# Gated product interleaved with a linear-attention recurrence: the split of x one step later, and a 0-3-3-2 pattern of gate halves

## The chip, the cores and the metric

The kernel runs on one core of one Trainium2 chip. The metric is device time in microseconds (us); of several runs the median is given. Engines are named as in the profile: PE (matrix products), PEld (its weight loads), DVE (vector), ACT (scalar), POOL (GpSimd), SP (the queue that issues most DMAs; ACT issues some as well).

## What is computed

There are 32 sequences (4 batches of 8 heads) of 768 positions and head size 48. Per sequence a recurrence with a decay per key channel is run, and its output, regrouped to 3072 tokens of 384 values, goes through a product of two linear maps and two more linear maps:

```python
for t in range(S):
    state = alpha[:, :, t, :, None] * state + np.einsum('bhd,bhe->bhde', k[:, :, t], v[:, :, t])
    y[:, :, t] = np.einsum('bhd,bhde->bhe', q[:, :, t], state)
...
x = y.transpose(0, 2, 1, 3).reshape(B * S, H * D)      # 3072 x 384
h = (x @ w1) * (x @ w2) @ w3                           # 1024 wide
out = h @ w_out                                        # 3072 x 384
```

## The kernel before

**Phase one** is the loop over `n` (steps 0 to 24). The 768 positions of a batch are six chunks of 128, so four batches make 24 chunks, one per step, for all eight heads at once. In step n PE does `attend_state(n - 1)` (L349), `scores(n)` (L330), `transposed(n + 1)` (L290), `attend(n - 1)` (L355), `outer(n)` (L302, not in a batch's last chunk) and `decays(n + 3)` (L253 or L256). ACT takes logarithms (L238), exponentials (L259, L260), copies transposed q and k out of PSUM (`qkT`, L292), copies the output y (L359) and issues its stores to the DRAM tile `xd` (L365). DVE masks the scores (`ms`, L333), scales q and k (`qk`, L268) and adds up states (L310, L312). Inputs are loaded three to five steps ahead by SP (L124, L130, L131, L136).

**Groups and gates.** Three chunks make a group g of 384 tokens. Once they are stored, `load_x(g)` (L370) brings them back transposed as `xT`, and `split_x(g, 0)` makes three parts `x3` of it: one ACT instruction (L376) and two DVE instructions (L377, L378), on 128x1152 elements each. There is one buffer of `xT`, and one of `x3` in phase one. `gate(g, f)` is one of eight column tiles of the product (x w1)(x w2): two halves, each `exact(...)` with six matmuls (L387), a copy on ACT (L389), three matmuls (L391) and a DVE instruction (L392); behind the second half DVE multiplies the two (`ab`, L403) and SP stores an earlier result (L410). The generators of gates stand in the queue `fill`, and `run(k)` emits k halves at its place in the step.

**Weights** arrive as 64-bit floats and are converted by generators that `convert(steps)` advances: a DMA into `raw` (L181), ACT instructions L189, L194 and L207, DVE instructions L190, L193, L196, L197, L199, L209 and L210. They fill ACT and DVE beside the recurrence.

**Order.** `begin = {4: group 0, 8: group 1, ... 20: group 4}` says in which step x of a group is loaded. For groups 0 to 3 four of the eight gates are put into `fill`, for group 4 all eight. The framework puts the instructions of each engine into one in-order stream by its own planning, so that an instruction can stand on its engine earlier or later than in the source; PSUM has eight banks, which all steps take in turn (`bank()`).

**Phase two** starts behind the loop: what is left in `fill`, then the remaining gates of all groups, with the conversion and folding of w3 and w_out (L430, L436), then 24 output tiles (`project`, L387 and L391 on `w3o`).

Of the kernel before, what the change touches and what calls it, by code (L numbers as in the profile page):

```python
# [48 lines left out]
def kernel(  # L49
# [71 lines left out]
    def load_a(n):  # L121
        if n < N:
            st["a", n] = inp.tile([C, H, D], FP32, tag="ac", name="ac")
            nc.sync.dma_start(out=st["a", n], in_=rows(alpha, n))  # L124

    def load_kq(n):
        if n >= N:
            return
        st["kq", n] = inp.tile([C, 2, H, D], FP32, tag="kq", name="kq")
        nc.sync.dma_start(out=st["kq", n][:, 0], in_=rows(k, n))  # L130
        nc.sync.dma_start(out=st["kq", n][:, 1], in_=rows(q, n))  # L131

    def load_v(n):
        if n < N:
            st["v", n] = vs[n % len(vs)]
            nc.sync.dma_start(out=st["v", n][:, :, 0:D], in_=rows(v, n))  # L136
# [77 lines left out]
    def convert(steps, ahead=3):  # L214

        for _ in range(steps):
            while weights and len(begun) < ahead:
                begun.append(weights.popleft())
                next(begun[-1])
            if not begun:  # L220
                return
            x = begun.popleft()
            try:
                next(x)
                begun.appendleft(x)
            except StopIteration:
                pass
# [5 lines left out]
    def logs(n):  # L233
        if n >= N:
            return
        a = st.pop(("a", n)).rearrange("p h d -> p (h d)")
        la = st["la", n] = work.tile([C, DM], FP32, tag="la", name="la")
        nc.scalar.activation(la, a, AF.Ln)  # L238
        if n >= LATE:

            t = st["la", n] = work.tile([C, 2, DM], FP32R, tag="la2", name="la2", bufs=1)
            nc.scalar.copy(t[:, 0], la)
            nc.vector.tensor_sub(t[:, 1], la, t[:, 0].bitcast(FP32))
        if n in ends:
            nc.scalar.dma_start(out=ends[n][2:3], in_=a[0:1])

    def decays(n):
        if n >= N:
            return
        lc = bank()[:, 0:DM]  # L250
        la = st.pop(("la", n))
        if n < LATE:
            nc.tensor.matmul(lc, utri if n % 2 else after, la, start=True, stop=True)  # L253
        else:
            for i in range(2):
                nc.tensor.matmul(lc, sums[:, n % 2], la[:, i], start=(i == 0), stop=(i == 1))  # L256

        e = st["e", n] = work.tile([C, 2, DM], FP32, tag="e", name="e", bufs=3)
        nc.scalar.activation(e[:, 0], lc, AF.Exp, scale=-1.0)  # L259
        nc.scalar.activation(e[:, 1], lc, AF.Exp)  # L260
        if n in ends:
            nc.scalar.dma_start(out=ends[n][0:1], in_=e[0:1, 0])
        if n + 1 in ends:
            nc.scalar.dma_start(out=ends[n + 1][1:2], in_=e[C - 1:C, 1])
# [14 lines left out]
    def transposed(n):  # L279
        if n >= N:  # L280
            return
        qk = qks[n % 3]
        qkT = work.tile([C, 2, NP, C], FP32, tag="qkT", name="qkT")

        tp = [bank().rearrange("p (i j c) -> p i j c", i=2, j=NP) for _ in range(2)]
        for i in range(2):
            for j in range(NP):
                for half in range(2):
                    s = ds(DP * half, DP)
                    nc.tensor.transpose(tp[half][:, i, j, :], qk[s, i, 2 * j:2 * j + 2, :], ident[s, s])  # L290
        for half in range(2):
            nc.scalar.copy(qkT[:, :, :, ds(DP * half, DP)], tp[half])  # L292
        st["qkT", n] = qkT
# [30 lines left out]
    def scores(n):  # L324
        qkT = st["qkT", n]
        sc = [bank().rearrange("p (j c) -> p j c", j=NP) for _ in range(2)]
        for j in range(NP):
            for i in range(2):
                r = ds(DP * i, D)
                nc.tensor.matmul(sc[i][:, j, :], qkT[r, 0, j, :], qkT[r, 1, j, :], start=True, stop=True)  # L330
        ms = work.tile([C, 2, NP, C], FP32, tag="ms", name="ms")
        for i in range(2):
            nc.vector.tensor_tensor(ms[:, i].bitcast(I32), sc[i].bitcast(I32), keep_bc, op=ALU.bitwise_and)  # L333
        st["ms", n] = ms
# [3 lines left out]
    def attend_state(n):  # L338
        qkT = st.pop(("qkT", n))

        y = [bank()[:, 0:HP * C].rearrange("p (j c) -> p j c", c=C) for _ in range(2)]
        st["y", n] = y, [(half * HP + j, i, y[i][ds(DP * half, DP), j, :])
                         for j in range(HP) for i in range(2) for half in range(2)]
        if n % NCH:
            for j, i, to in st["y", n][1]:
                r = ds(DP * i, D)
                nc.tensor.matmul(to, Ts[n % 2][r, j, :], qkT[r, 1, j, :],  # L349
                                 start=(j % HP == 0), stop=False, skip_group_check=True)  # L350
# [21 lines left out]
    def split_x(g, i):  # L372
        x = st.pop(("xT", g))
        t = tr[i].tile([C, 3, KM, TG], FP32R, tag="x3", name="x3")
        st["x3", g] = t
        nc.scalar.activation(t[:, 0], x, AF.Copy, scale=1.0 - 2.0 ** -13)  # L376
        nc.vector.tensor_sub(t[:, 1], x, t[:, 0].bitcast(FP32))  # L377
        nc.vector.scalar_tensor_tensor(t[:, 2], t[:, 0].bitcast(FP32), 1.0 + 1.0 / P, x,  # L378
                                       op0=ALU.mult, op1=ALU.subtract)

    def exact(to, w, x, scale):

        p1, p2 = (bank()[:, 0:to.shape[1]] for _ in range(2))
        n = len(w[0])
        for part in range(2):
            for i in range(n):
                nc.tensor.matmul(p1, w[part][i], x[part][i], start=(part == i == 0), stop=(part == 1 and i == n - 1))  # L387
        t = gw.tile(list(to.shape), FP32, tag="t", name="t")
        nc.scalar.activation(t, p1, AF.Copy, scale=(1.0 + 1.0 / P) * scale)  # L389
        for i in range(n):  # L390
            nc.tensor.matmul(p2, w[2][i], x[2][i], start=(i == 0), stop=(i == n - 1))  # L391
        nc.vector.scalar_tensor_tensor(to, p2, -scale, t, op0=ALU.mult, op1=ALU.add)  # L392

    def gate(g, f):
        r = []
        x = [[st["x3", g][:, part, kk, :] for kk in range(KM)] for part in range(3)]
        for i, scale in enumerate((1.0, P * P)):
            r.append(gw.tile([C, TG], FP32, tag="r", name="r"))
            exact(r[-1], [[w12[:, part, i, kk, ds(f * C, C)] for kk in range(KM)] for part in range(3)], x, scale)
            if len(r) == 1:  # L400
                yield
        ab = abp.tile([C, TG], FP32, tag="ab", name="ab")
        nc.vector.tensor_mul(ab, *r)  # L403
        store_ab()
        st["ab"] = g, f, ab

    def store_ab():
        if "ab" in st:
            g, f, ab = st.pop("ab")
            nc.sync.dma_start(out=abd[g][:, f, :], in_=ab)  # L410
# [57 lines left out]
    def run(pieces):  # L468

        for _ in range(pieces):  # L470
            if not fill:
                return
            try:
                next(fill[0])
            except StopIteration:
                fill.popleft()
# [18 lines left out]
    load_kq(3)  # L495
    load_a(4)

    begin = {4 + 4 * g: (g, range(FH if g < 4 else KF)) for g in range(5)}

    for n in range(N + 1):  # L500
        load_v(n + AHEAD - 1)
        load_a(n + 5)
        load_kq(n + AHEAD)
        if n:
            attend_state(n - 1)
        if n < N:
            scores(n)
        transposed(n + 1)
        if n - 1 in begin:
            g, tiles = begin[n - 1]  # L510
            split_x(g, 0)
            fill.extend(gate(g, f) for f in tiles)
        if n == 0:
            logs(2)
            decays(2)
            logs(3)
        early = n < 7
        convert(1, 2 if n == 0 else 3)
        advance(n)
        if n:  # L520
            attend(n - 1)
        outer(n)
        run(n - 1 not in begin)
        if early:
            convert(1)
        decayed(n + 2)
        logs(n + 4)
        if n in begin:
            load_x(begin[n][0], nc.scalar)
        convert(early and n > 2)  # L530
        run(1)
        decays(n + 3)
        load_ends(n + 2)
        convert(early or n % 3 == 0)
        run(n - 1 in begin)
    part1.close()


# [78 lines left out]
```

## Time and profile before

| | |
|---|---|
| median of 8 runs | 508.35 us (506.76 to 509.5) |
| profiled execution | 509.1 us |
| its span, first to last instruction | 507.3 us |
| mean granted PE clock | 0.966 |
| busy: PE, DVE, ACT | 467.7, 371.1, 248.4 us |
| HBM traffic | 56.40 MB read, 22.06 MB written |

A matmul's end is modelled, and matmuls overlap, so a busy PE is not PE at its peak. Busy shares are means over stages with different limits: phase one (to about 213 us) and phase two have to be read apart. In what follows, a row of a timeline gives start and length in us, the engine, the line of the kernel, the operation, output and inputs, shapes and the number of instructions merged; in square brackets stands the idle time of the engine just before and what ended it.

### The profile page before, as it was taken

To read this page: it belongs to the slowest core of one execution; us is meant where nothing else is said; L and a number is where in the kernel's file an instruction comes from. 1 tells how busy PE (TensorE), PEld (TensorE's weight loads), DVE (VectorE), ACT (ScalarE), POOL (GpSimd) and SP (SyncE) were. 2 spreads that over 40 slices of the span, in tenths; PEclk is the share of its full clock that TensorE was granted. 3 is DMA by queue.
4 is the path that set the end of the run, shared out by engine and by line. 5 is a ranking of instruction groups with operands and counts; after the bars stand their busy time and mean duration, and the time that the engine had idled before them with its cause. 6 is when DMAs were issued, how large, how long until landed. Compare 5 with 4: busy or idle time off the path is not lost.

```text
span 507.3 us, 9883 instructions
## 1 busy us (share of the span) xinstructions
PE 467.7 (92%) x3760; PEld 425.3 (84%) x3760; DVE 371.1 (73%) x620; ACT 248.4 (49%) x479; POOL 13.5 (3%) x43
## 2 busy tenths in 40 slices
PE   3778399499799999999999999999999999999997
PEld 1666288398698899899999998898888799999996
DVE  2778698699965767599999976967533496777771
ACT  2665566468656655355555554544323343333330
POOL 2000000010100000000000000000000000000000
PEclk9988599789899999999999999999999999999999
DMA  9999999998688843265555432332001686656511
GB/s 174 183 220 196 249 225 224 201 236 219 143 193 197 184 88 109 76 189 166 193 191 184 159 118 90 133 112 72 33 31 48 168 230 190 183 174 180 176 54 47
DMA packets 168735, 79.10 MB, mean 156 GB/s; under 512 B 112856, under 2 KB 162544, under 8 KB 168688
## 3 DMA queue, kind: packets, MB, share of 16 engines
q1 hardware_dynamic: 147184, 70.73, 54.3%
q10 hardware_dynamic: 21504, 7.75, 6.6%
q8 instruction: 29, 0.48, 0.4%
q14 instruction: 18, 0.15, 0.1%
HBM read 56.40 MB, written 22.06 MB: 155 GB/s over the span
## 4 chain that ended last, share of the span: by engine, by line
PE 66%; DMA 2%; ACT 2%; DVE 1%; issue 1%; ACTq 1%; DVEq 0%
PE bank L387 35%; PE bank L391 17%; PE bank L436 8%; PE bank L355 1%; PE bank L430 1%; PE bank L330 1%; DMA kq<-in_k_dram 1%; DMA raw<-in_moe_w_out_dram 1%; PE bank L349 1%; ACTq L365 1%; DVE x L378 1%; PE bank L290 0%; PE bank L302 0%; ACT qkT L292 0%; ACT t L389 0%
## 5 line engine op out<-in xcount | busy, mean ns | idle before, releaser
L387 PE MATMUL bank<-x,w 128*128 128x384 f32 x768 | 164.5, 349 | 18.1 <-ACT x L376 10.9
L387 PEld LDWEIGHTS bank<-x,w 128*128 128x128 f32 x768 | 136.6, 192 | 23.9 <-ACT x L376 11.3
L389 ACT ACTIVATE t<-bank 128x384 f32<-128x384 f32 x152 | 73.5, 490 | 119.1 <-PE bank L387 100.3
L392 DVE SCALAR_TENSOR_TENSOR r<-bank,t 128x384 f32<-128x384 f32 x128 | 68.8, 553 | 46.4 <-ACT t L389 37.2
L391 PE MATMUL bank<-x,w 128*128 128x384 f32 x384 | 89.6, 341 | 1.5 <-DVE x L378 1.4
L391 PEld LDWEIGHTS bank<-x,w 128*128 128x128 f32 x384 | 69.6, 192 | 3.1 <-PE bank L387 1.4
L387 PE MATMUL bank<-w3o,ab 128*128 128x384 f32 x384 | 70.6, 335 | 1.0 <-ACT ab L454 1.0
L387 PEld LDWEIGHTS bank<-w3o,ab 128*128 128x128 f32 x384 | 66.8, 188 | 1.4 <-ACT ab L454 1.3
L436 PE MATMUL bank<-wo,w3T 128*128 128x384 f32 x128 | 42.6, 486 | 0.0
L189 ACT ACTIVATE rest<-raw 128x512 f32<-128x512 uint32 (+1 forms) x36 | 23.4, 649 | 29.9 <-DMA raw<-in_moe_w_dram 17.1
L391 PE MATMUL bank<-w3o,ab 128*128 128x384 f32 x192 | 37.2, 334 | 0.0
L436 PEld LDWEIGHTS bank<-wo,w3T 128*128 128x128 f32 x128 | 24.2, 189 | 14.9
L403 DVE TENSOR_TENSOR ab<-r 128x384 f32<-128x384 f32 x64 | 35.4, 554 | 0.9
L455 DVE TENSOR_TENSOR ab<-abl,ab 128x1024 fp32r<-128x1024 f32 x24 | 29.3, 1222 | 8.6 <-ACT ab L454 8.6
L454 ACT ACTIVATE ab<-abl 128x1024 fp32r<-128x1024 f32 x24 | 25.5, 1062 | 20.1 <-PE bank L391 18.9
L333 DVE TENSOR_TENSOR ms<-bank,keep 128x512 int32<-128x512 int32 x48 | 31.2, 681 | 3.9 <-PE bank L330 3.9
L391 PEld LDWEIGHTS bank<-w3o,ab 128*128 128x128 f32 x192 | 33.6, 188 | 0.0
L330 PEld LDWEIGHTS bank<-qkT 48*128 48x128 f32 x384 | 24.7, 193 | 10.2 <-ACT qkT L292 4.8
L330 PE MATMUL bank<-qkT 48*128 48x128 f32 x384 | 29.8, 292 | 3.8 <-ACT qkT L292 3.3
L292 ACT COPY qkT<-bank 128x512 f32<-128x512 f32 x48 | 25.7, 586 | 13.9 <-PE bank L290 7.4
L392 DVE SCALAR_TENSOR_TENSOR o<-bank,t 128x384 f32<-128x384 f32 x24 | 13.4, 557 | 22.6 <-issue 12.9
L194 ACT ACTIVATE power<-power,rebias 128x512 uint32<-128x512 uint32 (+1 forms) x36 | 25.0, 695 | 9.9 <-DVE power L193 9.7
(65 smaller groups left out, 511.7 us busy)
## 6 DMA issues: line engine op xcount, KB each, us to landing
abd<-ab SPq DMA_DIRECT2D x64, 192.0 KB
abl<-abd SPq DMA_DIRECT2D x24, 512.0 KB
raw<-in_moe_w_dram SPq DMA_DIRECT2D x16, 512.0 KB
raw<-in_moe_w_dram SPq DMA_DIRECT2D x24, 256.0 KB
ac<-in_alpha_dram SPq DMA_DIRECT2D x24, 192.0 KB
kq<-in_k_dram SPq DMA_DIRECT2D x24, 192.0 KB
kq<-in_q_dram SPq DMA_DIRECT2D x24, 192.0 KB
v<-in_v_dram SPq DMA_DIRECT2D x24, 192.0 KB
```

The source lines that it names most:

```text
L194: nc.scalar.activation(power, power, AF.Relu, scale=2.0 ** 23, bias=rebias)
L292: nc.scalar.copy(qkT[:, :, :, ds(DP * half, DP)], tp[half])
L330: nc.tensor.matmul(sc[i][:, j, :], qkT[r, 0, j, :], qkT[r, 1, j, :], start=True, stop=True)
L333: nc.vector.tensor_tensor(ms[:, i].bitcast(I32), sc[i].bitcast(I32), keep_bc, op=ALU.bitwise_and)
L387: nc.tensor.matmul(p1, w[part][i], x[part][i], start=(part == i == 0), stop=(part == 1 and i == n - 1))
L389: nc.scalar.activation(t, p1, AF.Copy, scale=(1.0 + 1.0 / P) * scale)
L391: nc.tensor.matmul(p2, w[2][i], x[2][i], start=(i == 0), stop=(i == n - 1))
L392: nc.vector.scalar_tensor_tensor(to, p2, -scale, t, op0=ALU.mult, op1=ALU.add)
L403: nc.vector.tensor_mul(ab, *r)
L436: nc.tensor.matmul(po, w3T[:, j, :], wo[:, j, :], start=(j == 0), stop=(j == KF - 1))
L454: nc.scalar.activation(t[:, 0], ab, AF.Copy, scale=1.0 - 2.0 ** -13)
L455: nc.vector.tensor_sub(t[:, 1], ab, t[:, 0].bitcast(FP32))
```

## The change

The step in which x is split and its gates are put into the queue is n - 2, not n - 1, behind the load. In each step from 6 on, the number of gate halves follows from n: none in the split step, then three, three and two. Before it was two in every step. `run` is called at the same three places of the step.

```diff
-        if n - 1 in begin:
-            g, tiles = begin[n - 1]
+        if n - 2 in begin:
+            g, tiles = begin[n - 2]
             split_x(g, 0)
             fill.extend(gate(g, f) for f in tiles)
+        pieces = (0, 3, 3, 2)[(n - 6) % 4] if n > 5 else 0
...
         outer(n)
-        run(n - 1 not in begin)
+        run(pieces > 0)
...
         convert(early and n > 2)
-        run(1)
+        run(pieces > 1)
         decays(n + 3)
         load_ends(n + 2)
         convert(early or n % 3 == 0)
-        run(n - 1 in begin)
+        run(pieces > 2)
```

## The prediction

> **What bounds the kernel now.** I read the page first, then the time-sliced windows, the waits of PE, and last the timelines of PE, ACT and DVE around the waits that the change aims at.
>
> The page says that PE is busy for 467.7 of 507.3 us, and the windows say where the rest is.
>
> ```profile
> PE 467.7 (92%) x3760; PEld 425.3 (84%) x3760; DVE 371.1 (73%) x620; ACT 248.4 (49%) x479; POOL 13.5 (3%) x43
> ...
> 33.92:40.75 6.83, 5.61 (x54) 4.36 (x58) 6.83 (x12) 4.23 (x10) 0.00 (x0) 0.50 1.18 221
> 51.00:64.64 13.64, 5.52 (x13) 3.93 (x14) 9.08 (x15) 7.46 (x15) 0.00 (x0) 0.50 1.06 248
> 66.66:128.12 61.46, 54.31 (x656) 48.78 (x652) 53.75 (x99) 40.10 (x88) 3.44 (x6) 0.92 0.99 219
> 140.15:198.68 58.53, 57.46 (x755) 52.84 (x751) 40.05 (x68) 35.03 (x79) 3.18 (x9) 1.00 0.67 157
> 213.00:507.00 294.00, 289.70 (x1586) 271.53 (x1582) 215.10 (x348) 125.43 (x212) 0.00 (x0) 1.00 0.43 136
> ```
>
> Columns of a window: stretch, length, busy time of PE, PEld, DVE, ACT and POOL, granted PE clock, DMA share, GB/s. From 140 us on PE is full at clock 1.00: there only less PE work helps, and the change removes none. All that can be won lies before 140, where DVE (53.75 of 61.46) and the DMA engines (share 0.99) are nearly full too. The waits of PE and the timeline show what is lost:
>
> ```profile
> PE bank L387 <- ACT x L376: 10.9, 2, 9.7
> PE bank L387 <- DVE x L377: 7.2, 3, 4.9
> ...
> 48.01 1.09 PE L355 MATMUL bank<-ms,v 128*64 128x128 f32 x16
> 58.84 1.33 PE L387 MATMUL bank<-x,w 128*128 128x384 f32 x3 [9.73 <-ACT x L376]
> ...
> 94.07 0.79 PE L387 MATMUL bank<-x,w 128*128 128x384 f32 x3 [1.17 <-ACT x L376]
> 99.75 1.33 PE L387 MATMUL bank<-x,w 128*128 128x384 f32 x3 [4.89 <-DVE x L377]
> ...
> 134.07 0.79 PE L387 MATMUL bank<-x,w 128*128 128x384 f32 x3 [2.09 <-DVE x L377]
> 135.43 0.76 PE L391 MATMUL bank<-x,w 128*128 128x384 f32 x3 [0.57 <-DVE x L378]
> ...
> 167.64 0.76 PE L391 MATMUL bank<-x,w 128*128 128x384 f32 x3 [0.83 <-DVE x L378]
> ```
>
> In each group's split step the first gate half reaches PE before the split of x is done: 9.98 us for group 0 (9.73 and the 0.25 that follows at 60.41), 6.06 for group 1, 2.66 for group 2, 0.83 for group 3, none for group 4. After the first three the clock is 0.50, over 5.8, 5.85 and 3.4 us of PE work, which costs half of it: 2.9, 2.9 and 1.7. Together 27.0 us. That is the ceiling, not the gain, as two more lines show:
>
> ```profile
> 54.73 0.66 ACT L189 ACTIVATE rest<-raw 128x512 f32<-128x512 uint32 x1 [4.73 <-DMA xT<-xd]
> 57.12 0.61 ACT L292 COPY qkT<-bank 128x512 f32<-128x512 f32 x1
> 95.00 0.43 DVE L190 TENSOR_SCALAR mant<-raw 128x512 uint32<-128x512 uint32 x1 [4.23 <-DMA raw<-in_moe_w_dram]
> ```
>
> At the first stall ACT itself stands for 4.73 us, until a transfer has landed, and only then copies qkT of step 6 (done 57.73), which the scores of step 6 need whatever the gates do. At the second stall DVE stands for 4.23 us for a weight tile; the split at 98.35 is only behind that in its queue.
>
> **The change part by part.** Units, from the timeline of step 10 (105.77 to 113.09 us): a gate half is 1.67 and 1.56, mean 1.62 us of PE; a step without gates is 3.66 plus 0.44 for the sums of logarithms, 4.1 us. The split is ACT 1.17 and DVE twice 1.35 (starts 1.27 apart).
>
> *The split a step later.* No instruction is added or removed; the two DVE and one ACT instructions go behind one more step of recurrence on those queues, past its copies, its masks and its xd stores. The split issues no DMA; in the built order the load of x for group 1 also moves, from behind the e of step 7 to step 8, so it starts later by some of the slack won. SP and POOL lose or gain no instruction in phase one except that stores of ab move with their gates. From load to first gate half there is, in the source, about one step before and two and a half after.
>
> *The split step without gates.* Between the last gate of a group and the first of the next lie 4.1 us more of PE work, which covers the chain of 1.17 + 1.27 + 1.35 = 3.8 us that must wait for the single x3 buffer. With that cover gone it costs what it costs now (2.66 at group 2).
>
> *Three, three, two halves.* 8 halves per four steps stay 8, at 4.1 + 3 x 1.62 = 9.0 us of PE in a full step. Of group 4 three gates instead of four fit in phase one: 38 halves instead of 40, so two (3.24 us) are moved into phase two, which PE bounds; they are subtracted below. There five gates instead of four (16 us) stand ahead of the first split of phase two, which needs 3.8: no cost.
>
> *Sum up to the scores of step 13* (128.12 us now, 16 halves done; then T, 14 done; gain 128.12 - T - 3.24). The scores of step 6 start at 57.7 instead of 66.66. From there two bounds. DVE: its instructions of steps 6 to 12, at the distances of their starts, are 51.7 us in the new order (55.6 in the old: one split more, two weight conversions fewer); with the old idle time (63.6 us from the masks of step 6 to those of step 13, 55.9 busy, so 7.7 idle) from the end of the scores at 58.9 it is at step 13's masks at 118.3; less the old lag of 3.4 behind the scores, T = 114.9: gain 10.0. DMA at its old rate: 13.46 MB (219 GB/s x 61.46) plus 2.1 of the 8.9 us that are skipped (236 GB/s), less two weight tiles and one store, 1.1 MB, is 14.5 MB or 66 us: T = 123.8, gain 1.1. PE itself would need 7 x 4.1 + 14 x 1.62 = 51.4 us and is not the bound. I take 4.0, below the middle of the two, because the DMA share of 0.99 is nearer to full than DVE's 0.87.
>
> *Sum from step 13 on.* Groups 2 and 3 lose 2.66 + 1.7 + 0.83 = 5.2 and some 0.3 of slow restart, 5.5. In its place come three steps without gates (14, 18, 22). Such steps ran early in the trace: scores at 21.85 and 26.36, at 41.19 and 46.03, so 4.5 and 4.8 us undisturbed, 0.6 above the work of 4.1. Three make 1.8: gain 3.7. DVE, which gets the two conversions (7.4 us) here, has 18 us idle in 140.15 to 198.68. The other end: the same three steps at 9.0 us, as from 32.20 to 41.19, would cost 14.7 and lose 9.2; at no cost they gain 5.5.
>
> Sum: 4.0 + 3.7 = 7.7 us. The profiled execution took 509.1 us (1.8 around its span), so 501.4; the median of the 8 runs is 0.75 lower, so I forecast **500.7 us**.
>
> **The rivals.** *The transfers keep the pace.* Up to step 13 nothing is won (the DMA row's 1.1 or less, with wait and weight tile found again one instruction later); only 3.7 remains: 504.7. For it: share 0.99, and DMA waits on ACT and DVE at both large stalls. Against: in the stretch where PE stood, 48 to 54 us, DMA moved 258 GB/s, so it can go faster than 219.
>
> *The waits go and nothing replaces them.* 10.0 + 5.5 = 15.5: 492.9. Against it: every early step without gates had some gap.
>
> *Slower: the steps without gates stop the clock.* In 33.92 to 40.75, recurrence without gates, the clock was 0.50 although the gap just before was only 1.78 us:
>
> ```profile
> 35.14 1.12 PE L290 MATMUL bank<-ident,qk 64*128 64x64 f32 x16 [1.78 <-DVE qk L268]
> ```
>
> One such trip costs the gap, 1.8, and half of the 5.61 us of PE work, 2.8: 4.6. In the new order DVE has 5.3 us in step 14 (masks 1.2, second half of the split 1.27, state 0.27, qk 0.87, a conversion's end 1.2, logarithms 0.47) against PE's 4.1. If nothing is won early and two of the three late steps trip, 5.5 - 9.2 = -3.7: 512.0. It decides at two trips; at one it is still a small gain. Against it: in steps 1 and 2 (20 to 30 us) gaps of 0.48 left the clock at 1.00, and DVE is 68% busy after 140.
>
> [...]
>
> *The stall only changes place.* Split and raw tile stay in one DVE queue, and PE waits for masks or qk as long as it did for x: within 0.3%.
>
> **How the numbers follow.** A measurement of this kernel tells about 0.3%, 1.5 us, from no change. Forecast (497 to 503.5) 0.47; transfers keep the pace (504.7) 0.20; all waits go (492.9) 0.08; same place 0.06; slower 0.19. The first three are faster: 0.75. Low end 494.5, which leaves out about half of the third case; high end 510, which leaves out most of the slower one, together under 2 in 10.
>
> **What would show it.** Right: the waits of L387 and L391 for x (19.5 us) under 3; scores of step 6 near 58 us, of step 7 near 64; DVE's 4 us stand for a raw tile still there with PE going on; scores of step 13 near 121; clock 1.00 after 140; PE over 95% busy in the steps 14, 18 and 22. Wrong: scores of step 13 later than 124 (transfers), or 0.50 stretches beside the steps without gates (slower), or new waits of L290 and L330 for qk and qkT of over 8 us, or PE idle at the start of phase two.

## The result, and the profile after

The changed kernel takes **503.71 us** (median of 11 runs, 502.07 to 506.76) beside 508.41 of the kernel before (32 runs): a ratio of 0.9918 (95% interval 0.99 to 0.9936), 4.7 us faster. Its profiled execution took 503.4 us, its span is 501.6, the mean granted clock 0.983.

Of the page, the row of busy times; then stretches with the columns explained above. The first five lie in phase one, the last is phase two.

```profile
PE 469.7 (94%) x3760; PEld 428.1 (85%) x3760; DVE 371.5 (74%) x620; ACT 249.2 (50%) x479; POOL 12.5 (2%) x43
```

```profile
33.92:40.75 6.83, 5.52 (x94) 4.33 (x92) 6.83 (x13) 4.82 (x11) 0.00 (x0) 1.00 1.12 212
...
58.06:68.30 10.24, 8.13 (x82) 6.39 (x78) 8.71 (x15) 7.24 (x15) 0.00 (x0) 0.50 1.01 228
55.60:120.18 64.58, 56.04 (x637) 49.66 (x637) 52.70 (x92) 39.33 (x88) 2.70 (x6) 0.92 1.04 223
...
136.57:139.98 3.41, 3.01 (x38) 2.92 (x38) 3.41 (x7) 2.13 (x6) 0.40 (x2) 0.50 0.80 145
...
140.15:198.68 58.53, 57.36 (x749) 52.83 (x746) 44.65 (x78) 34.73 (x79) 2.85 (x7) 1.00 0.63 153
213.00:501.00 288.00, 285.00 (x1557) 267.41 (x1555) 209.37 (x336) 122.03 (x204) 0.00 (x0) 1.00 0.43 135
```

The first row lies ahead of the first split, where PE runs the same instructions in the same order as before; its clock was 0.50 before and is 1.00 here, so two executions can differ by a stop of the clock that the change did not make. The third row runs from the scores of step 6 to those of step 13. The DMA engines are as full as before (share 1.04, before 0.99) and moved 223 GB/s (before 219); DVE is busy for 52.70 of 64.58. The clock is 0.50 in 47.82 to 51.24, in the second row, and again in the fourth, beside the split of group 2; the kernel before has such a stretch there too, from 136.32 to 139.74. PE's waits (total, times, longest):

```profile
PE bank L290 <- DVE qk L268: 8.3, 6, 3.4
PE bank L330 <- ACT qkT L292: 5.6, 4, 2.6
PE bank L253 <- ACT la L238: 4.8, 2, 4.4
PE bank L290 <- ACT t L389: 2.6, 1, 2.6
PE bank L349 <- DVE ms L333: 1.8, 2, 1.0
PE bank L349 <- ACT e L260: 1.8, 1, 1.8
PE bank L387 <- DVE ms L333: 1.2, 1, 1.2
```

No row names x any more: the 19.5 us are gone. But qk rose from 5.6 to 8.3, qkT from 3.3 to 5.6, and four rows are new or larger. ACT and DVE still stand for the transfers. What these two wait for over the whole execution, in the same form, for ACT (first row) and DVE of the changed kernel, and then of the kernel before:

```profile
ACT rest L189 <- DMA raw<-in_moe_w_dram: 22.1, 13, 2.9
```

```profile
DVE mant L190 <- DMA raw<-in_moe_w_dram: 9.4, 5, 3.8
```

```profile
ACT rest L189 <- DMA raw<-in_moe_w_dram: 17.1, 8, 2.8
```

```profile
DVE mant L190 <- DMA raw<-in_moe_w_dram: 14.2, 4, 4.5
```

The sum of the two rows was 31.3 us and is 31.5. Much of it lies ahead of the change: from 40 to 215 us, all waits of ACT and DVE that are put down to a transfer sum to 26.1 us before and 25.6 after. The change took the wait out of PE's way in one place, and did not shorten it. At the first split, on ACT, DVE and PE:

```profile
52.52 0.68 ACT L189 ACTIVATE rest<-raw 128x512 f32<-128x512 uint32 x1 [2.89 <-DMA raw<-in_moe_w_dram]
...
53.92 0.43 DVE L190 TENSOR_SCALAR mant<-raw 128x512 uint32<-128x512 uint32 x1 [2.20 <-DMA raw<-in_moe_w_dram]
...
54.92 0.61 ACT L292 COPY qkT<-bank 128x512 f32<-128x512 f32 x1
...
55.58 1.16 PE L330 MATMUL bank<-qkT 48*128 48x128 f32 x16 [1.45 <-ACT qkT L292]
...
57.63 0.84 PE L290 MATMUL bank<-ident,qk 64*128 64x64 f32 x16 [0.89 <-DVE qk L268]
...
66.31 1.35 DVE L378 SCALAR_TENSOR_TENSOR x<-x,xT 128x1152 fp32r<-128x1152 f32 x1
...
69.99 1.33 PE L387 MATMUL bank<-x,w 128*128 128x384 f32 x6 [1.19 <-DVE ms L333]
```

ACT stands for 2.89 us (before 4.73), copies qkT 2.2 us earlier than before, and the scores of step 6 start at 55.58 instead of 66.66. The first gate half starts at 69.99, 2.3 us after the split is done at 67.66; what it waits for last is a mask. PE's gaps here are small and many where they were one of 9.73 us, and the clock is still 0.50 for 10.24 us.

**Where the time went, by steps.** The trace gives the starts of the scores and the halves between them. "Lost" is the length from the scores of step 13 to those of step 23 less 10 x 4.1 and 1.62 for each half, the units of the prediction. All times in us.

| kernel | scores of 13 | halves before | 13 to 23 | halves | lost | from 23 to the end |
|---|---|---|---|---|---|---|
| before | 128.12 | 16 | 78.16 | 20 | 4.8 | 301.03 |
| changed | 120.18 | 14 | 75.53 | 18 | 5.4 | 305.91 |
| split shift alone | 122.71 | 14 | 77.31 | 20 | 3.9 | 302.80 |
| pattern alone | 121.81 | 16 | 80.31 | 19 | 8.5 | 302.78 |
| changed, half the weight bytes | 116.46 | 14 | 71.86 | 18 | 1.7 | 306.11 |
| changed, weights held back | 120.25 | 14 | 73.42 | 18 | 3.3 | 305.94 |
| changed, one half in step 14 | 122.40 | 14 | 75.68 | 18 | 5.5 | 305.91 |
| changed, DVE relieved | 118.12 | 14 | 78.33 | 18 | 8.2 | 305.91 |
| changed, decay transfers on POOL | 120.73 | 14 | 75.57 | 18 | 5.4 | 306.00 |
| 1, 3, 2, 2 halves | 122.54 | 14 | 75.25 | 19 | 3.5 | 304.54 |
| 1, 3, 2, 2 and weights held back | 120.80 | 14 | 73.55 | 19 | 1.8 | 304.35 |
| split shift and weights held back | 123.28 | 14 | 78.79 | 20 | 5.4 | 302.80 |
| before, half the weight bytes | 116.20 | 16 | 76.95 | 20 | 3.6 | 301.03 |

Each row is one execution; the experiment with one half in step 14 shows below that single step times repeat to some 2 us only.

The span of the profiled execution became 5.7 us shorter, while the medians differ by 4.7. Up to step 13 the gain is 128.12 - 120.18 - 3.24 (two halves fewer) = 4.7. From 13 to 23 the loss beside the work rose by 0.6. From 23 on the changed kernel has four halves more (6.48) and takes 4.88 longer: 1.6 gained. Of these, 1.0 is the one wait of PE for ab (L387 for L454) in phase two of before, which has no row after. 4.7 - 0.6 + 1.6 = 5.7.

### The profile page after: what moved, and what is told of

Read it like the earlier page. It is cut to its first block, busy times and chain, and to the rows that moved or that the text cites. A ratio compares the mean times of both kernels' runs of the same rounds, so it can differ in the third digit from the quotient of the medians.

```text
span 501.6 us, 9876 instructions
## 1 busy us (share of the span) xinstructions
PE 469.7 (94%) x3760; PEld 428.1 (85%) x3760; DVE 371.5 (74%) x620; ACT 249.2 (50%) x479; POOL 12.5 (2%) x43
## 3 DMA queue, kind: packets, MB, share of 16 engines
q1 hardware_dynamic: 147184, 70.73, 55.6%
HBM read 56.40 MB, written 22.06 MB: 156 GB/s over the span
## 4 chain that ended last, share of the span: by engine, by line
PE 73%; DMA 10%; DVE 9%; ACT 2%; SPq 2%; issue 2%; ACTq 1%; DVEq 0%
PE bank L387 37%; PE bank L391 18%; PE bank L436 8%; DMA raw<-in_moe_w_dram 6%; PE bank L330 3%; PE bank L355 2%; DMA ac<-in_alpha_dram 2%; PE bank L430 1%; PE bank L290 1%; DMA xd<-x 1%; DVE mant L199 1%; DMA v<-in_v_dram 1%; DVE ms L333 1%; PE bank L349 1%; DVE power L197 1%
## 5 line engine op out<-in xcount | busy, mean ns | idle before, releaser
L387 PE MATMUL bank<-x,w 128*128 128x384 f32 x768 | 159.0, 341 | 1.3 <-DVE ms L333 1.2
L387 PEld LDWEIGHTS bank<-x,w 128*128 128x128 f32 x768 | 134.0, 188 | 5.2 <-DVE ms L333 1.6
L389 ACT ACTIVATE t<-bank 128x384 f32<-128x384 f32 x152 | 74.1, 491 | 128.9 <-PE bank L387 94.8
L391 PE MATMUL bank<-x,w 128*128 128x384 f32 x384 | 87.3, 334 | 0.0
L387 PE MATMUL bank<-w3o,ab 128*128 128x384 f32 x384 | 70.4, 334 | 0.0
L391 PEld LDWEIGHTS bank<-x,w 128*128 128x128 f32 x384 | 68.5, 188 | 0.0
L387 PEld LDWEIGHTS bank<-w3o,ab 128*128 128x128 f32 x384 | 66.9, 188 | 0.0
L330 PEld LDWEIGHTS bank<-qkT 48*128 48x128 f32 x384 | 27.5, 208 | 13.7 <-ACT qkT L292 8.8
L330 PE MATMUL bank<-qkT 48*128 48x128 f32 x384 | 32.9, 308 | 6.0 <-ACT qkT L292 5.6
L454 ACT ACTIVATE ab<-abl 128x1024 fp32r<-128x1024 f32 x24 | 25.5, 1062 | 19.0 <-PE bank L391 18.8
L290 PE MATMUL bank<-ident,qk 64*128 64x64 f32 x384 | 19.8, 248 | 11.8 <-DVE qk L268 8.3
L355 PE MATMUL bank<-ms,v 128*64 128x128 f32 x384 | 30.1, 302 | 0.3 <-ACT e L260 0.3
```

What stands on the lines that cost most here:

```text
L355: nc.tensor.matmul(to, vc[:, 2 * j + i, :], ms[:, i, j, :], start=(n % NCH == 0 and j % HP == 0), stop=(j % HP == HP - 1), skip_group_chec ...
L454: nc.scalar.activation(t[:, 0], ab, AF.Copy, scale=1.0 - 2.0 ** -13)
```

## The experiments

My theory was that the change works through both its parts: the later split takes the wait away, and the step without gates covers the split. The rivals were that one part does it all, that DVE is the bound, and that the transfers are.

**The split two steps behind the load, nothing else.** Two halves in every step, as before.

```diff
-        if n - 1 in begin:
-            g, tiles = begin[n - 1]
+        if n - 2 in begin:
+            g, tiles = begin[n - 2]
...
-        run(n - 1 not in begin)
+        run(n - 2 not in begin)
...
-        run(n - 1 in begin)
+        run(n - 2 in begin)
```

> The later split alone: x is split two steps behind its load, but every step keeps two gate halves, in the split step too. Theory (the step without gates is what covers the chain of 3.8 us through the one x3 buffer; the longer way behind the load helps group 0 alone): PE's waits for x fall only at group 0, from 19.5 us to 7 to 10 in all, and the time is 505 to 507 us. Rival (it is the time between load and split that was short): the waits for x all but vanish and the time is 503 us or less, since 40 halves instead of 38 lie in phase one.

503.28 us (4 runs), ratio 0.9893 (0.9874 to 0.9912): as fast as the whole change. Its waits for x:

```profile
PE bank L391 <- DVE x L378: 3.7, 2, 1.9
PE bank L387 <- ACT x L376: 2.9, 1, 2.9
PE bank L387 <- DVE x L377: 2.1, 1, 2.1
```

8.7 us of waits for x are left, inside the theory's 7 to 10, and it is no slower for them. The theory's time, 505 to 507 us, did not come. So the claim that the step without gates is needed fell: the shift alone gives all of the gain.

**The pattern of halves alone**, with the split one step behind the load.

```diff
+        pieces = (0, 3, 3, 2)[(n - 5) % 4] if n > 4 else 0
...
-        run(n - 1 not in begin)
+        run(pieces > 0)
...
-        run(1)
+        run(pieces > 1)
...
-        run(n - 1 in begin)
+        run(pieces > 2)
```

> The pattern alone: x is split one step behind its load as before, but with no gates in that step (5, 9, 13, 17, 21) and three, three and two halves in the next three. Theory (the step without gates is the part that works): waits for x under 4 us, 503 to 505 us. Rival (the distance to the load is the part that works): group 0 still waits some 8 us, and the time is 506 to 508.5 us.

505.77 us (12 runs), ratio 0.9944 (0.992 to 0.9967), between the two expected ranges, with no wait for x at all. It has the scores of step 13 at 121.8 with two halves more than the changed kernel, so the early part won 6.3 us; then the clock is 0.50 in 130.0 to 136.8 and in 164.1 to 167.5, and 13 to 23 lost 8.5 us, 3.8 more than before. That is the slower rival's case of two stops, with its price of 9.2 near to what came, but against an early gain that the rival had put at nothing. The parts do not add: by the ratios 1.07% and 0.56% alone, 0.82% together.

**DVE relieved**: the changed kernel without the instructions that handle the exponent of a weight (L193, L194 and L197 go, L196 and L199 become one), about 1.5 us less of DVE for each weight tile.

```diff
-        nc.vector.tensor_scalar(power, high, 20, 0x7FF, ...)
-        nc.scalar.activation(power, power, AF.Relu, ...)
...
-        nc.vector.scalar_tensor_tensor(mant, top, 2.0 ** -20, rest, ...)
-        nc.vector.scalar_tensor_tensor(power, high, 0x80000000, power, ...)
...
-        nc.vector.tensor_mul(to, mant, power.bitcast(FP32))
+        nc.vector.scalar_tensor_tensor(to, top, 2.0 ** -20, rest, op0=ALU.mult, op1=ALU.add)
```

> The changed kernel with less DVE and ACT work in the weight conversion: exponent and sign are left out (L193, L194, L197 and L199 go), so the weights are wrong by a power of two; the transfers stay as they are. It takes 1.5 us of DVE and 0.6 us of ACT from each of 36 conversions. Theory (transfers set the pace up to step 13): the scores of step 13 stay within 3 us of 120.2; the half-clock stretch at step 14 goes, and the time is 499 to 501.5 us. Rival (DVE sets the pace there): the scores of step 13 come at 111 to 115 us and the time is 493 to 496 us.

505.75 us (5 runs), ratio 0.9942 (0.9916 to 0.9967): no faster than with that work. Up to step 13 the scores are 2.1 us earlier (118.12), which the stretch behind gives back; the clock was 0.50 in 137.8 to 141.2 all the same, so the expectation for step 14 was wrong. DVE is busy for 47.4 us less in all (324.1 for 371.5), and its waits for weight tiles rose from 9.4 to 20.3 us: what it saved it stood. The amount of DVE work is not what sets the time; the order of its queue still matters, for the longest of PE's waits for DVE in this kernel, 4.7 us, is for one mask.

**The transfers relieved**: the changed kernel, each weight tile loaded in half and read twice.

```diff
-        raw = rawp.tile([C, n], I64, tag="raw", name="raw")
+        raw = rawp.tile([C, n // 2], I64, tag="raw", name="raw")
...
-            nc.sync.dma_start(out=raw[:, ds(i * m, m)], in_=src)
+            nc.sync.dma_start(out=raw[:, ds(i * m // 2, m // 2)], in_=src[:, 0:m // 2])
```

> The changed kernel with half of the weight bytes: each conversion loads half of its columns and uses them twice, so half of the weights are wrong; the arithmetic stays as it is. It takes 0.25 MB from each of 12 conversions of w1 and w2 and as much in proportion from the others. Theory (transfers set the pace up to step 13): some 2.5 MB less before step 13, at 219 GB/s 11 us, bounded by DVE: scores of step 13 at 111 to 116 us, time 496 to 500 us. Rival (DVE sets the pace): scores of step 13 at 118 to 121, time 502 to 504 us.

496.57 us (4 runs), ratio 0.9763 (0.9747 to 0.9779). Instructions and shapes on the engines are those of the changed kernel; 8.9 MB less are read (47.48 for 56.40), and 7.1 us go: in the profiled execution 3.7 up to step 13, and 3.7 between 13 and 23, where no clock of 0.50 shows and the loss beside the work is 1.7 us. Of the two resources, the transfers are the one whose relief shortens the time. But the scores of step 13, at 116.46, come just behind the expected 111 to 116: up to there some 2.7 MB less were moved (199 GB/s for 116.46 us, in the changed kernel 215 for 120.18), which would be 12 us at 219 GB/s, and 3.7 came. So the transfers are not the only bound there, and DVE's relief, with 2.1 us up to step 13, is not told from them by this stretch alone. The two largest rows of PE's waits that are left, in this kernel's line numbers (three more than above), are for qk and for one mask:

```profile
PE bank L293 <- DVE qk L271: 6.6, 5, 3.7
PE bank L256 <- DVE ms L336: 4.7, 1, 4.7
```

**The same relief in the kernel before.**

> The kernel before, with half of the weight bytes (each conversion loads half of its columns and uses them twice, so half of the weights are wrong). Theory (late transfers are what the old order stumbled over, the split only stood behind them): the waits for x fall to under 8 us of 19.5, the time to 497 to 499.5 us, and against 496.6 of the changed kernel with the same relief the change is worth under 3 us. Rival (the chain of the split itself is too short in the old order): the waits for x stay above 12 us, the time is 500.5 to 502.5 and the change is worth 4 to 6 us here too.

497.40 us (4 runs), ratio 0.9793 (0.9763 to 0.9823). The waits for x did not fall as expected: 12.4 us are left, the rival's number. But the time is within 0.8 us of the relieved changed kernel's; by the ratios, each to the kernel before on its own chip, the two differ by 0.3%, 1.5 us, with intervals that overlap. The relief is worth 11 us here and 7.1 in the changed kernel. Once the weights come in time, 12 us of waits for x make no difference that can be measured; most of the 4.7 us that the change is worth, it is worth through late transfers.

**Another spread**: 1, 3, 2, 2 halves.

```diff
-        pieces = (0, 3, 3, 2)[(n - 6) % 4] if n > 5 else 0
+        pieces = (1, 3, 2, 2)[(n - 6) % 4] if n > 5 else 0
...
-        run(pieces > 0)
+        run(pieces > 1)
...
-        run(pieces > 2)
+        run(pieces in (1, 3))
```

> The changed kernel with one, three, two and two halves instead of none, three, three and two: the split step gets a half at its end. Theory (with transfers setting the pace, the spread of the halves hardly matters once the split is a step later): 502.5 to 504.5 us, within 1 us of the changed kernel and of the split alone (503.3). Rival (an empty step starves PE at step 14 and a full one behind it wastes cover, a half in it repairs that): the half-clock stretch at step 14 goes and the time is 500 to 502 us.

503.34 us (6 runs), ratio 0.9904 (0.9878 to 0.993). No clock of 0.50 at step 14, as the rival had it, but one at 90.0 to 93.4, and the time of the changed kernel, as the theory had it: the spread matters little by itself.

**The weights held back**: one advance of the conversion less per step in steps 7 to 13, one more behind.

```diff
-        convert(1, 2 if n == 0 else 3)
+        convert(n < 7 or n > 13, 2 if n == 0 else 3)
...
-        convert(early or n % 3 == 0)
+        convert(early or n > 13 or n % 2)
```

> The changed kernel with the conversions of w1 and w2 held back: none to one instead of one to two advances per step in steps 7 to 13, two in steps 14 to 24; all arithmetic stays. In the built order two weight loads move from before the loads of step 15 to behind them. Theory (transfers set the pace up to step 13): 1 MB less before step 13, 3 to 5 us at 219 GB/s, of which half may come back in steps 14 to 20: 500.5 to 502.5 us. Rival (the weight loads only wait where nobody needs them): 503 to 504.5 us.

502.72 us (6 runs, 499.88 to 504.76), ratio 0.9897 (0.9863 to 0.9931): between the two expected ranges, and not told apart from the changed kernel. Up to step 13 nothing was won (120.25 for 120.18), against the theory; the 2.1 us that this execution is better between 13 and 23 come with a clock of 1.00 there.

**The small transfers of the decays issued by POOL** instead of ACT. In the changed kernel ACT stands for 3.59 us at 86 to 89.85, and issues one of them (L276 at 88.54) just before t (L389); PE stands for 2.65 us with it. The row of t puts the wait down to a load of alpha.

```diff
-            nc.scalar.dma_start(out=ends[n][0:1], in_=e[0:1, 0])
+            nc.gpsimd.dma_start(out=ends[n][0:1], in_=e[0:1, 0])
```

(and so at L245, L264 and L276)

> The changed kernel with the small DMAs of the decay ends (L245, L262, L264, L276, 40 of 1.5 to 2.2 KB) issued by POOL instead of ACT. In the changed kernel PE stands 2.65 us at 87.7 us behind a copy on ACT that stood behind such an issue, and ACT stands before 52.2 us behind another. Theory (these issues hold ACT): the 2.65 us go, and the scores of step 6 come 1 to 3 us earlier; 500.5 to 502.5 us. Rival (ACT waits for weight tiles there anyway): 503 to 504.5 us; slower if POOL's own issue is slow enough to make the decay late.

504.38 us (6 runs), ratio 0.9921 (0.9892 to 0.995): nothing won. The scores of step 6 come at 51.9, 3.7 us earlier, those of step 7 at 61.7 as before. PE's wait of 2.65 us is gone; one of 1.8 us of L349 for POOL is new, and others for qkT. The time is in the rival's range.

**One half in step 14**: steps 14 to 17 run 1, 3, 2, 2, all others as in the change.

```diff
-        pieces = (0, 3, 3, 2)[(n - 6) % 4] if n > 5 else 0
+        pieces = ((1, 3, 2, 2) if 14 <= n < 18 else (0, 3, 3, 2))[(n - 6) % 4] if n > 5 else 0
...
-        run(pieces > 0)
+        run(pieces > 1)
...
-        run(pieces > 2)
+        run(pieces > 2 or pieces == 1)
```

> The changed kernel with one group of steps altered: steps 14 to 17 run 1, 3, 2, 2 gate halves in place of 0, 3, 3, 2; everything else, steps 6, 10, 18 and 22 without gates included, stays. This tries the term of the sum that was mis-sized: if the late steps came out at 1.0 us in place of 3.7 because the gateless step 14 stopped the clock, then with one half in step 14 there is no clock of 0.50 between 125 and 145 us, the scores of step 18 start 2 to 4 us earlier than 162.1 (about 159), and the time is 2 to 4 us below the changed kernel's 503.7: 500 to 501.7. Rival: the clock halves once wherever the transfers leave a gap of some us, and work taken out of one place waits in the next; then the scores of step 13 or 18 move by less than 1 us in sum and the time is 502.7 to 504.5, as the spread 1, 3, 2, 2 in all groups gave 503.3.

506.21 us (12 runs), ratio 0.9949 (0.9926 to 0.9971): not faster. There is no clock of 0.50 between 125 and 145 us, and the scores of step 18 come 39.0 us behind those of step 13 instead of 41.9, so the piece of 2.9 us is won there, as the theory had it. It is lost again in the next step without gates, 18, and the one behind it (16.7 us for 13.6). On PE and DVE:

```profile
163.04 1.35 DVE L377 TENSOR_TENSOR x<-xT,x 128x1152 fp32r<-128x1152 f32 x1
...
164.78 1.28 DVE L333 TENSOR_TENSOR ms<-bank,keep 128x512 int32<-128x512 int32 x2
165.98 1.35 DVE L378 SCALAR_TENSOR_TENSOR x<-x,xT 128x1152 fp32r<-128x1152 f32 x1
166.44 1.16 PE L330 MATMUL bank<-qkT 48*128 48x128 f32 x16 [1.07 <-ACT qkT L292]
...
167.52 0.95 DVE L268 TENSOR_TENSOR qk<-kq,e 128x768 f32<-128x768 f32 x1
...
168.61 0.94 PE L290 MATMUL bank<-ident,qk 64*128 64x64 f32 x16 [1.01 <-DVE qk L268]
```

From 168.9 to 172.3 the clock is 0.50. The rival's picture, that work taken out of one place waits in the next, fits; its numbers do not: 506.21 us lies above both expected ranges, and the step times moved by more than its 1 us. In this kernel the instructions of PE, DVE and ACT stand in the same order as in the changed one up to step 14, and yet the scores of step 13 come 2.2 us later (122.40 for 120.18): single step times of one execution are known to some 2 us, no better.

**Two attempts at a better version**: the spread 1, 3, 2, 2 with the weights held back, and the split shift alone with the weights held back. Their edits are those shown above, put together.

> Meant to beat both kernels: the spread of 1, 3, 2, 2 halves together with the weights held back (in steps 7 to 13 the first advance of the conversion of weights is left out; behind step 13 one advance more per step). Held back alone with 0, 3, 3, 2 it gave 502.7, spread alone 503.3. Theory (transfers set the pace, about 1 us each is to be had, and they add): 501 to 502.5. Rival (both only move the same gap): 502.7 to 504.

> Meant to beat both kernels with less: the split two steps behind the load with two halves in every step (503.3 alone), and the weights held back as in the other. Theory: the waits for x that were left at groups 0 and 1 (8.7 us) keep what the held-back weights free, so 502.5 to 503.5, no better than the changed kernel. Rival: with fewer weight tiles between 66 and 125 us ACT and DVE come to the split sooner, the waits fall under 5 us, and the time is 500 to 502.

The first takes **501.64 us** (6 runs, 500.48 to 502.95) beside 508.93 of the kernel before on its chip (17 runs), ratio 0.9862 (0.9837 to 0.9888). The interval lies below that of the changed kernel (0.99 to 0.9936): it beats both, by as much as the expectation said. It is not told apart from the split shift alone (0.9874 to 0.9912) or the weights held back (0.9863 to 0.9931), and it is the best of the eight variants here that compute the whole result, so some of its lead may be chance. Between 13 and 23 it loses 1.8 us beside its work, and its clock is 1.00 from 70.6 to 497 us. The second takes 504.75 us (6 runs), ratio 0.9921 (0.9892 to 0.9949), above the theory's number; 10.7 us of waits for x are left in it, so the rival, which wanted them under 5, is out. Holding the weights back won nothing beside the shift alone (503.28), so that the two parts of the first kernel add is not shown.

## Why the prediction was right, and where not

The forecast was 500.7 us, range 494.5 to 510; 503.71 is inside, and the sign is right. By its steps:

- **The waits for x go, scores of steps 6, 7 and 13 near 58, 64 and 121.** Right: none is left, and the scores came at 55.6, 61.8 and 120.2.
- **Gain up to step 13: 4.0, between the row of the DMA (1.1) and that of DVE (10.0).** Measured 4.7, and 2.5 in the kernel of the same order: the size holds, and leaning to the DMA row was right for the time as a whole. Halving the weight bytes won 7.1 us, taking DVE's work away nothing. That the number fits so closely is in part luck: neither relief moved the scores of step 13 as far as its row would have it. The DMA rate rose by 2% only (219 to 223 GB/s), and the stretch began 2.1 us earlier than the 57.7 that the ACT row gave.
- **DVE's stand for a raw tile stays, with PE going on.** In part: from 40 to 215 us DVE's waits for raw tiles of `in_moe_w_dram` fell from 8.8 to 5.6 us, while ACT, which had none of these there, stood 4.7 us for them; PE went on in small pieces, at clock 0.50.
- **Two halves moved, no cost at phase two's first split.** Right: no PE wait there, and the stretch from 23 on came out 1.6 us better than the halves account for; the 1.0 of it that is the wait for ab was not foreseen.
- **From step 13 on: 3.7 = 5.5 less 3 x 0.6.** This term failed. From 13 to 23 the change lost 0.6 instead of winning 3.7; with the 1.6 behind it, 1.0 is left. The mis-sized part is the price of the three steps without gates, 1.8 forecast, 5.2 measured; the loss that it replaces was 4.8 by the table's units, not 5.5. The 0.3 of slow restart in that 5.5 is a term that no run shows; the named waits and half of the work at clock 0.50 are 5.2. I had taken the 0.6 from the two shortest early steps without gates (4.5 and 4.8 us; the others took 5.8, 6.7 and 9.0, the last of which the prediction names as the other end) and called them undisturbed. Steps 18 and 22 took 4.45 and 4.08 us, 0.35 and nothing beyond their 4.1. Step 14 with the one behind it, to the scores of step 16, took 17.9 against 4.1 + 9.0 = 13.1 of work: 4.8. The windows from the scores of step 14, 15, 18 and 22 to the next:

```profile
128.35:135.07 6.72, 4.97 (x87) 3.96 (x83) 6.72 (x12) 5.08 (x11) 0.00 (x0) 1.00 0.71 181
135.07:146.26 11.19, 10.45 (x111) 9.69 (x109) 9.12 (x18) 5.90 (x16) 1.43 (x3) 0.85 0.93 197
162.06:166.51 4.45, 3.68 (x70) 3.23 (x67) 4.45 (x6) 3.49 (x9) 0.00 (x0) 1.00 0.61 182
191.62:195.70 4.08, 3.73 (x84) 3.39 (x81) 4.04 (x6) 2.30 (x5) 0.00 (x0) 1.00 0.15 52
```

On PE and DVE:

```profile
131.89 1.34 DVE L377 TENSOR_TENSOR x<-xT,x 128x1152 fp32r<-128x1152 f32 x1
132.40 0.62 PE L256 MATMUL bank<-la,sums 128*128 128x384 f32 x2
133.16 1.27 DVE L333 TENSOR_TENSOR ms<-bank,keep 128x512 int32<-128x512 int32 x2
133.98 1.16 PE L349 MATMUL bank<-qkT,T 48*64 48x128 f32 x16 [0.96 <-DVE ms L333]
134.35 1.34 DVE L378 SCALAR_TENSOR_TENSOR x<-x,xT 128x1152 fp32r<-128x1152 f32 x1
135.07 1.16 PE L330 MATMUL bank<-qkT 48*128 48x128 f32 x16
135.62 0.34 DVE L312 TENSOR_TENSOR T<-bank,T 128x192 f32<-128x192 f32 x1
135.89 0.94 DVE L268 TENSOR_TENSOR qk<-kq,e 128x768 f32<-128x768 f32 x1
...
136.97 1.12 PE L290 MATMUL bank<-ident,qk 64*128 64x64 f32 x16 [0.74 <-DVE qk L268]
138.02 1.97 PE L355 MATMUL bank<-ms,v 128*64 128x128 f32 x16
```

DVE is busy for all 6.72 us of step 14. In its queue the masks stand behind the first half of the split and qk behind the second: PE waits for 0.96 and 0.74 us, and from 136.57 the clock is 0.50 (L355 takes 1.97 instead of 1.09). The rival of the stopped clock had this mechanism and its place (DVE's work against PE's 4.1 in step 14: 5.3 forecast, 6.7 found, since nearly all of both halves of the split and the end of a gate fall into it). Its price, 4.6 for 4.8, is close by luck, from other terms: 2.5 us of idle PE and half of the 3.01 us of work at clock 0.50, 1.5, with 0.8 not accounted for, where it had 1.8 and 2.8. What it had wrong is the count, two for one, and the early gain, none for 4.7.

The clock is only a part of this price. In the kernel with the weights held back, steps 14 and 15 run the same halves at clock 1.00 and still take 16.4 us, 3.3 beyond their work; with half the weight bytes it is 2.0 and with the decay transfers on POOL 2.2, again at 1.00. So without a stop these two steps lose 2.0 to 3.3 us, and 1.5 to 2.8 is left for the stop, as an estimate from single executions. Nor does a clock that holds make the term come true: of the five kernels of the table whose clock is 1.00 from step 13 to step 23 and that have steps of none or one half, two lose 1.7 and 1.8 us beside their work, and three lose 3.3, 3.5 and 5.4. I should have given DVE's queue in step 14, and one stop, a place in the sum.

- **The reason for the gain.** I had put it on both parts of the change and on the cover of a step without gates. The shift alone gave 503.28, so the pattern adds nothing that can be measured beside it. Why the two do not add is not settled beyond this: with the weights in time the whole change is worth 0.8 us by the times and 1.5 by the ratios, neither clear of noise.
- **PE over 95% busy in steps 14, 18 and 22.** Wrong: by the windows above 74, 83 and 91%. The clock is 1.00 after 140, as said.
- **Wrong if L290 and L330 wait over 8 us more.** These rows rose by 2.7 + 2.3 = 5.0, in the direction of that sign, short of it.
- **Wrong if the clock is 0.50 beside the steps without gates.** This sign came, beside steps 6 and 7 (58.06 to 68.30) and behind step 14, though the time stayed in the range.
- **The row behind the rival of the stopped clock.** I read the gap of 1.78 us that ends at 35.14 as what brought the clock down. It begins at 33.36 and the clock falls at 33.92, so only 0.56 us of it lie before.

## What to carry to other kernels

An engine's wait for an operand that stands in the queue behind a late transfer was worth here what the transfer left when the operand was moved: 19.5 us of named waits went, 4.7 us came. Try the relief of the transfers (half the bytes) and of the suspected engine (fewer instructions) before a schedule is tuned; here they gave 7.1 us and nothing. When filler work is taken from a step, compare what each helper engine has in that step with what is left on the bound engine, and price the gaps of the bound engine first and then a stop of its clock, here, as an estimate, half of the work in a stretch of 3.41 to 13.65 us.

## What the runs showed of the hardware

The clock fell to 0.50 at 136.57 us. Before that PE had gaps of 0.72 and 0.96 us, and one of 0.74 us that had begun 0.34 us earlier. In the kernel before, it fell at 33.92 us behind gaps of 0.44 and 0.56 us. The sum of the gaps does not tell a fall from none. In the kernel with the weights held back, at the same place:

```profile
129.55 0.71 PE L290 MATMUL bank<-ident,qk 64*128 64x64 f32 x15 [0.53 <-DVE r L392]
...
133.25 0.76 PE L349 MATMUL bank<-qkT,T 48*64 48x128 f32 x16 [0.96 <-DVE ms L333]
...
136.25 0.71 PE L290 MATMUL bank<-ident,qk 64*128 64x64 f32 x16 [1.14 <-DVE qk L268]
```

Here 2.63 us of gaps within 7.2 us left the clock at 1.00 (L355 takes 1.09 us at 130.19 and at 136.89); in the changed kernel it fell beside 2.42 us of gaps within 7.4, 2.02 of them ahead of the fall.

In the traces of the kernel before and of the changed one, the clock falls seven times between 30 and 140 us (the last column takes as long a time ahead as the shortest of the stretches lasts):

| kernel | clock 0.50 from | for | PE busy in the 3.41 us ahead |
|---|---|---|---|
| before | 33.92 | 6.83 | 2.41 |
| before | 50.99 | 13.65 | 1.52 |
| before | 95.36 | 10.24 | 1.74 |
| before | 136.32 | 3.41 | 1.68 |
| changed | 47.82 | 3.41 | 1.64 |
| changed | 58.06 | 10.24 | 1.59 |
| changed | 136.57 | 3.41 | 2.18 |

With the weights held back, PE is busy for 1.86 of the 3.41 us that end at 136.25, less than ahead of two of these falls, and the clock stays at 1.00. So neither figure decides by itself; no run set out to test what does.
